# Query pieces two batches ahead, keys one pair earlier, K turned in front of the key additions, in a fused attention and mixture-of-experts kernel

## The chip, the cores and the metric

The kernel runs on one NeuronCore of one Trainium2 chip. The metric is the device time of one execution in microseconds (us): the median of three runs. The profile is of one further execution, taken by the hardware profiler; its span, from the first to the last instruction, is some us shorter than the device time. TensorE is PE in the profile (its weight loads PEld), VectorE is DVE, ScalarE is ACT, GpSimd is POOL, SyncE is SP.

## The reference

Attention with one key and value head for 16 query heads, and then a two-level mixture of experts in which each token takes one expert.

```python
def _attn_ref(q, k, v):                      # q (8,16,384,64), k and v (8,1,384,64), float32
    scores = np.matmul(q, k.transpose(0, 1, 3, 2)) / np.sqrt(64)
    scores = scores - np.max(scores, axis=-1, keepdims=True)
    attn = np.exp(scores)
    attn = attn / (np.sum(attn, axis=-1, keepdims=True) + 1e-09)
    return np.matmul(attn, v)

def _moe_ref(x, w_group, w_expert, w1, w2):  # x (3072,1024); 4 groups of 4 experts; w1, w2 (4,4,1024,1024)
    # g = argmax(x @ w_group), g_w = its softmax weight; e = argmax(x @ w_expert[g]), e_w likewise
    # out[token] = g_w * e_w * relu(x @ w1[g, e]) @ w2[g, e]
```

The rows of x are the tokens: batch times 384 positions, with the 16 heads of 64 laid side by side.

## The kernel before

**Pairs.** Attention is done in 24 pairs `p` of a batch and a block of 128 query positions: `b, st = divmod(p, 3)`, `st` 0, 1 or 2. The loop over `p` (line 501) writes out by hand the order of the instructions of every engine; an engine's instructions run in that order, each when its semaphores allow. I call the work of one turn of the loop the phase of pair p. A phase has three parts.

- *Head*: three key blocks of scores (`scores(p, 0)` to `scores(p, 2)`, line 242: four matmuls of K against Q into a PSUM tile, then one exponential on ACT into a tile `pt`), and `prep_q(p + 1)` (line 238): one DVE transpose that turns the next pair's queries, as they lie in `qraw`, into `qT`.
- *Middle*: for six key blocks `j`, the value matmuls of the pair before (`values(p - 1, j)`, line 280), the scores that remain, the DVE key additions `pre_add` (line 253) that sum the exponentials over key blocks, `join` and `invert` for the reciprocals of the sums, and `stats_q(p)` (line 204) on ACT, which reads `qraw`. After that `weigh(p - 1)` (line 292) multiplies the values by the reciprocals, casts them on POOL to `xbf`, and after a batch's last pair has SP store `xbf` to `x_bf` in DRAM. `fold_keys(p)` (line 260) ends DVE's work on the pair.
- *Fills*: `fill(1)` four times, five times in pairs 8, 12, 16, 20 and 22 (line 554). Each pops one of the 14 expert units of an earlier batch: eight `h_unit`s (line 407: 8 matmuls with `w1`, one ReLU on ACT) and six `y_unit`s (line 415: 8 matmuls with `w2`, one ACT instruction that scales by `gsel` into a tile `y`, one SP store of `y` to the output). `y` has four buffers, so the fifth `y` in a row waits until the first one's store has landed. All these, and the scores, take turns on three PSUM buffers (`ps_s`, `tag="s"`).

**Expert choice.** In the fills of `st == 1` the gate's logits of batch b are made (`gate_a`, `gate_both`), in those of `st == 2` `counts(b, b - 1)` (line 334): two small matmuls, then on DVE `choose_b(b)` (line 349: `top` and its index on line 352, from which POOL requests the batch's expert weights `w1` and `w2`, lines 143 and 357), and `gate_c(b - 1)` (line 389), whose last result `gsel` (line 400) every `y_unit` of batch b - 1 reads. On DVE these stand behind `fold_keys(p)` and `prep_k`, and ahead of the next pair's `prep_q`.

**Transfers of queries and keys.** `load_q(b)` (line 82) takes one of two `qraw` buffers and puts eight pieces of 192 KB on a list `q_todo`; `some_q()` (line 95) requests one. SP requests them on line 89, in runs of 128 bytes. Before the change `load_q(b + 1)` is called at the start of the phase with `st == 0`. Up to p = 3 four pieces go out in the middle of a phase, later one after each fill. So a later batch's first pieces are requested in the fills of `st == 0` and the rest in those of `st == 1`. `prep_q` of that batch's first pair needs all eight, and it stands at the head of the phase with `st == 2`. `load_k(b)` (line 100) requests the keys in four pieces of 48 KB, also in runs of 128 bytes, and `prep_k(b)` (line 228) turns them on DVE into `kT[b]`, which the first scores of the next batch read. Before, keys are requested behind the middle of `st == 1` and turned behind `fold_keys` of `st == 2`. SP has one queue for all of these and for the stores of `y` and `x_bf`; it takes them in the order of the program.

**Tail.** After the last pair, lines 571 to 721 do the remaining expert units and one pair of batch and expert that the choice left out, gathered to at most 128 rows.

Of the kernel before, what the change touches and what calls it, by code (L numbers as in the profile page):

```python
# [21 lines left out]
def kernel(  # L22
# [12 lines left out]
    B, H, S, D = q.shape  # L35
# [6 lines left out]
    ST = S // P  # L42
# [39 lines left out]
    def load_q(b):  # L82
        t = pool.tile([P, HP, NB, 32], FP32, tag="qraw", bufs=2, name="qraw")
        q_raw[b] = t
        n = HP // 2

        def piece(i, a, j):
            hs = slice(i * n, (i + 1) * n)
            nc.sync.dma_start(out=t[64 * a + 32 * j:64 * a + 32 * j + 32, hs].rearrange("p h k d -> p (h k) d"), in_=qv[b, a, j, :, hs].rearrange("i h k d -> i (h k) d"))
        for i in range(2):  # L90
            for a in range(2):
                for j in range(2):
                    q_todo.append(lambda i=i, a=a, j=j: piece(i, a, j))
# [6 lines left out]
    def load_k(b):  # L100
        kt = pool.tile([P, NB, 32], FP32, tag="k", bufs=2, name="k")
        for a in range(2):
            for j in range(2):
                nc.sync.dma_start(out=kt[64 * a + 32 * j:64 * a + 32 * j + 32], in_=kv[b, 0, j])
        k_raw[b] = kt
# [98 lines left out]
    def stats_q(p):  # L204
        junk = pool.tile([P, 2 * CW], BF16, tag="junk", bufs=1, name="junk")
        nc.scalar.activation(out=junk[:].rearrange("p (h n) -> p h n", h=HP), in_=q_of(p), func=ACTF.Square, accum_out=stat_q[:, p:p + 1])  # L206

    def stats_k(b):
        junk = pool.tile([P, 2 * CW], BF16, tag="junk", bufs=1, name="junk")
        nc.scalar.activation(out=junk[:, 0:S], in_=k_raw[b][:].rearrange("p k d -> p (k d)" if b > 0 else "p s a d -> p (s a d)"), func=ACTF.Square, accum_out=stat_k[:, b:b + 1])  # L210
# [8 lines left out]
    def turn_q(p, nat, copies):  # L219
        qT[p] = pool.tile([P, 2 * CW], FP32, tag="qT", bufs=2, name="qT")  # L220
        n = HP // len(copies)
        for i, copy in enumerate(copies):
            ps = side([P, 2 * CW], FP32, "qps")
            for h in range(n):
                nc.tensor.transpose(out=ps[:, h * P:(h + 1) * P], in_=nat(i * n + h).rearrange("p a d -> p (a d)"), identity=ident[:])
            copy(out=qT[p][:, i * n * P:(i + 1) * n * P], in_=ps[:, 0:n * P])

    def prep_k(b):
        kT[b] = pool.tile([P, S], FP32, tag="kT", name="kT")
        nc.vector.transpose(out=kT[b][:], in_=k_raw[b][:].rearrange("p k d -> p (k d)"))  # L230

    def q_of(p):
        b, st = divmod(p, ST)
        if b == 0:
            return q_raw[0][:, st].rearrange("p h a d -> p h (a d)")
        return q_raw[b][:, :, st * (P // 32):(st + 1) * (P // 32)].rearrange("p h k d -> p h (k d)")

    def prep_q(p):
        qT[p] = pool.tile([P, 2 * CW], FP32, tag="qT", bufs=2, name="qT")
        nc.vector.transpose(out=qT[p][:].rearrange("p (h n) -> p h n", h=HP), in_=q_of(p))  # L240

    def scores(p, j):
        b = p // ST
        ps = side([P, 2, CW], FP32, "s")
        for c in range(2):
            for a in range(2):
                r = slice(64 * a, 64 * a + 64)
                nc.tensor.matmul(out=ps[64 * c:64 * c + 64, a, :], lhsT=kT[b][r, j * D:(j + 1) * D], rhs=qT[p][r, c * CW:(c + 1) * CW], start=True, stop=True)  # L248
        t = pool.tile([P, 2, CW], FP32, tag="pt", bufs=9, name="pt")
        nc.scalar.activation(out=t[:], in_=ps[:], func=ACTF.Exp, scale=scale)  # L250
        pt[p, j] = t

    def pre_add(p, j):
        if j == 1:
            presum[p] = pool.tile([P, 2, CW], FP32, tag="presum", bufs=1, name="presum")
            nc.vector.tensor_add(out=presum[p][:], in0=pt[p, 0][:], in1=pt[p, 1][:])  # L256
        else:
            nc.vector.tensor_add(out=presum[p][:], in0=presum[p][:], in1=pt[p, j][:])  # L258

    def fold_keys(p):  # L260
        fold[p] = pool.tile([P, 32], FP32, tag="fold", name="fold")
        nc.vector.tensor_reduce(out=fold[p][:], in_=presum[p][:].rearrange("p a (n i) -> p (a n) i", i=32), axis=AX, op=OP.add, apply_transpose=True)  # L262
    sums = {}

    def join(p):
        sm = side([P, 2, CW], FP32, "sm")
        for c in range(2):
            for a in range(2):
                r = slice(64 * c, 64 * c + 64)
                nc.tensor.matmul(out=sm[64 * a:64 * a + 64, c, 0:16], lhsT=sel2[r].rearrange("p a b -> p (a b)"), rhs=fold[p][r, 16 * a:16 * a + 16], start=True, stop=True)  # L270
        sums[p] = sm
# [8 lines left out]
    def values(p, j):  # L280
        b = p // ST
        if j == 0:
            o_ps[p] = ps_m.tile([P, 2, CW], FP32, tag="o", name="o")
        for c in range(2):
            for a in range(2):
                r = slice(64 * c, 64 * c + 64)
                nc.tensor.matmul(out=o_ps[p][64 * a:64 * a + 64, c, :], lhsT=v_sb[b][r, j, :], rhs=pt[p, j][r, a, :], start=(j == 0), stop=(j == KB - 1))  # L287
# [169 lines left out]
    def fill(n):  # L457
        while n > 0:
            if not units:
                if begun[0] >= B or begun[0] not in wts:  # L460
                    return
                units.extend(first_units(begun[0]))
                begun[0] += 1
            units.pop(0)()
            n -= 1
# [7 lines left out]
    def jobs_gates(b):  # L473
        if b == 0:
            return [lambda: gate_a(0, 0, 1), lambda: choose_a(0, gate_b(0, 0, 1)), lambda: counts(0, None)]
        return [lambda: gate_a(b, 0, ST), lambda: gate_both(b)]
# [24 lines left out]
    for p in range(NP):  # L501
        b, st = divmod(p, ST)
        jobs = jobs_gates(0) if p == 2 else []
        if st == 0 and b + 1 < B:
            load_q(b + 1)
        for j in range(3):
            scores(p, j)
            if p == 0 and j == 0:
                turn_q(1, lambda h: q_raw[0][:, 1, h], [nc.vector.tensor_copy])
        if p == 0:  # L510
            prep_k(1)
        elif 2 < p < NP - 1:
            prep_q(p + 1)
        if jobs:
            jobs.pop(0)()
        if p == ST + 1:
            fill(3)
        for j in (1, 2):
            pre_add(p, j)
        for j in range(KB):  # L520
            if p > 0:
                values(p - 1, j)
            if j == 2 and p > 0:
                join(p - 1)
            if j + 3 < KB:
                scores(p, j + 3)
            if 0 < j < 4:
                pre_add(p, j + 2)
            if j == 2 and p > 0:
                invert(p - 1)  # L530
            if j == 3:
                stats_q(p)
                if p == 1:
                    turn_q(2, lambda h: q_raw[0][:, 2, h], [nc.scalar.copy])
                elif p == 2:
                    turn_q(3, lambda h: q_nat[h // HC][:, h % HC], [nc.scalar.copy])
            if jobs:
                jobs.pop(0)()
            if p <= ST and 0 < j < 5:
                some_q()  # L540
        assert not jobs
        if p > 0:
            weigh(p - 1)
        fold_keys(p)
        if st == 1 and b + 1 < B:
            if b > 0:
                load_k(b + 1)
            load_v(b + 1)
        if st == 2 and b + 1 < B:
            if b > 0:  # L550
                prep_k(b + 1)
            stats_k(b + 1)
        if p > ST:
            n = 5 if p in FIVES else 4
            steps = {}
            if st == 2 and b > 0:
                steps = {0 if b == 1 else 1: lambda: counts(b, b - 1)}
            if st == 1:
                gate_a_, gate_b_ = jobs_gates(b)
                steps = {n - 2: gate_a_, n - 1: gate_b_}  # L560
                if b == B - 1:
                    steps = {1: gate_a_, 2: gate_b_, n - 1: lambda: counts(b, b - 1)}
            if p == NP - 1:
                steps = {1: bound_a, 2: bound_b}
            for i in range(n):
                fill(1)
                some_q()
                if i in steps:
                    steps[i]()
# [256 lines left out]
```

## Time and profile before

| | |
|---|---|
| device time, median of 3 | 499.33 us (499.28 to 500.36) |
| span of the profiled execution | 495.7 us |
| mean granted TensorE clock | 0.985 |
| PE busy | 467.5 us (94%) |
| DVE busy | 304.4 us (61%) |
| ACT busy | 248.0 us (50%) |
| query pieces, 56 of 192 KB | median 5.0 us from request to landing |
| key pieces, 28 of 48 KB | median 3.4 us |
| stores of `y`, 36 of 256 KB | median 5.6 us |
| stores of `x_bf`, 8 of 768 KB | median 7.8 us |
| expert weights | 4 transfers of 512 KB, 10.1 us, and 1 of 2048 KB, 24.2 us, for a batch |

An engine that is busy nearly all the span sets the time, and then its idle stretches are what can be taken away without changing its work. So the table is to be read together with the list of who waited for whom, and with the order in time around each of PE's gaps. Transfers run beside all engines; what counts is what waits for their landing.

### The profile page before, as it was taken

The numbers are of one execution on the slowest core, as the hardware profiler recorded it, in microseconds if no ns is written. First come the engines' busy times: TensorE is split into PE (matmuls) and PEld (weight loads), VectorE is DVE, ScalarE is ACT, GpSimd is POOL, SyncE is SP. The second block draws the span as 40 slices with busy tenths as digits, with TensorE's granted clock in tenths as the row PEclk, the third lists the DMA queues.
The fourth block names the chain that finished last, engine by engine and source line by source line (L and its number), as shares of the span: only waits on it lengthen the run. The fifth ranks groups of instructions, "written<-read, shape, count | busy, mean of one in ns | idle before, by whom it ended". The sixth has DMA issues, their size and how long they took to land. (4 is left out here: it accounts for less than half of the span.)

```text
span 495.7 us, 9385 instructions
## 1 busy us (share of the span) xinstructions
PE 467.5 (94%) x3810; PEld 203.9 (41%) x3828; DVE 304.4 (61%) x479; ACT 248.0 (50%) x355; POOL 60.3 (12%) x82
## 2 busy tenths in 40 slices
PE   8999999999979999697999999899997999999994
PEld 6333343344433343232344434344433434444652
DVE  4999759757397454781678671985449774834210
ACT  3957546554626546253465455455463465423332
POOL 1003000300012000300003000020003101202000
PEclk9999999999999999798999999999999999999998
DMA  9889991699609996299734998089961992994991
GB/s 166 95 108 154 217 184 13 124 243 225 100 2 183 252 188 70 35 199 267 159 33 61 226 240 166 1 137 240 188 128 19 195 212 108 182 223 133 228 242 69
DMA packets 155746, 74.52 MB, mean 150 GB/s; under 512 B 120731, under 2 KB 139163, under 8 KB 155696
## 3 DMA queue, kind: packets, MB, share of 16 engines
q0 software_dynamic: 28512, 37.84, 44.4%
q1 hardware_dynamic: 126384, 35.81, 34.6%
q8 instruction: 32, 0.52, 0.4%
q10 hardware_dynamic: 800, 0.20, 0.2%
q14 instruction: 18, 0.15, 0.1%
HBM read 92.62 MB, written 19.40 MB: 226 GB/s over the span
## 5 line engine op out<-in xcount | busy, mean ns | idle before, releaser
L250 ACT ACTIVATE pt<-s 128x1024 f32<-128x1024 f32 x144 | 141.9, 1026 | 71.3 <-PE s L248 70.1
L248 PE MATMUL s<-qT,kT 64*64 64x512 f32 x1152 | 146.7, 609 | 16.2 <-DVE top L352 12.0
L287 PE MATMUL o<-pt,v 64*64 64x512 f32 x1152 | 142.1, 594 | 0.0
L258 DVE TENSOR_TENSOR presum<-presum,pt 128x1024 f32<-128x1024 f32 x96 | 116.6, 1215 | 16.9 <-ACT pt L250 11.4
L412 PE MATMUL hps<-xbf,w 128*128 128x384 bf16 x512 | 89.0, 326 | 2.2 <-ACT hT L413 1.6
L420 PE MATMUL yps<-w,hT 128*128 128x512 bf16 x367 | 85.6, 379 | 0.9
L287 PEld LDWEIGHTS o<-pt,v 64*64 64x64 f32 x1152 | 44.2, 134 | 77.4 <-issue 77.1
L248 PEld LDWEIGHTS s<-qT,kT 64*64 64x64 f32 x1152 | 40.8, 135 | 79.9 <-issue 52.9
L299 POOL CAST xbf<-xT 128x1024 bf16<-128x1024 f32 x24 | 25.0, 1043 | 355.6 <-DVE xT L298 355.6
L412 PEld LDWEIGHTS <-w 128*128 128x128 bf16 x512 | 48.2, 98 | 47.6 <-issue 18.2
L413 ACT ACTIVATE hT<-hps 128x384 bf16<-128x384 f32 x64 | 31.4, 491 | 70.1 <-PE hps L412 64.7
L256 DVE TENSOR_TENSOR presum<-pt 128x1024 f32<-128x1024 f32 x24 | 29.1, 1211 | 50.8 <-ACT pt L250 50.5
L420 PEld LDWEIGHTS <-hT 128*128 128x128 bf16 x384 | 36.4, 98 | 47.9 <-issue 7.3
L421 ACT ACTIVATE y<-yps,gsel 128x512 f32<-128x512 f32 x36 | 24.4, 687 | 55.5 <-PE yps L420 37.1
L240 DVE STREAM_TRANSPOSE qT<-qraw 128x1024 f32<-128x1024 f32 x20 | 24.5, 1225 | 22.6 <-DMA qraw<-in_q_dram 22.6
L298 DVE TENSOR_TENSOR xT<-o,rinv 128x1024 f32<-128x1024 f32 x24 | 29.2, 1216 | 4.2 <-PE o L287 4.2
L277 DVE STREAM_TRANSPOSE rinv<-rc 128x1024 f32<-128x1024 f32 x24 | 29.9, 1246 | 0.8
L143 POOL DMA_DIRECT2D w<-in_moe_w_dram x36 | 24.8, 707 | 41.9 <-DVE gsel L400 22.0
L262 DVE TRANSPOSE_TENSOR_REDUCE fold<-presum 128x32 f32<-128x1024 f32 x24 | 29.6, 1232 | 0.0
L364 DVE COPY L<-lps 128x20 f32<-128x20 f32 (+1 forms) x16 | 3.0, 186 | 40.6 <-PE lps L318 40.6
L206 ACT ACTIVATE junk<-qraw 128x1024 bf16<-128x1024 f32 x21 | 22.0, 1048 | 0.0
L421 ACT ACTIVATE yt<-yps,gsel 128x512 f32<-128x512 f32 x12 | 8.2, 687 | 15.6 <-PE yps L420 12.0
(147 smaller groups left out, 187.3 us busy)
## 6 DMA issues: line engine op xcount, KB each, us to landing
w<-in_moe_w_dram POOLq DMA_DIRECT2D x36, 512.0 KB, 10.1
w<-in_moe_w_dram POOLq DMA_DIRECT2D x9, 2048.0 KB, 24.2
qraw<-in_q_dram SPq DMA_DIRECT2D x56, 192.0 KB, 5.0
out_dram<-y SPq DMA_DIRECT2D x36, 256.0 KB, 5.6
x_bf<-xbf SPq DMA_DIRECT2D x8, 768.0 KB, 7.8
out_dram<-yt SPq DMA_DIRECT2D x12, 256.0 KB, 6.2
v<-in_v_dram SPq DMA_DIRECT2D x16, 96.0 KB, 2.8
k<-in_k_dram SPq DMA_DIRECT2D x28, 48.0 KB, 3.4
```

The source lines that it names most:

```text
L248: nc.tensor.matmul(out=ps[64 * c:64 * c + 64, a, :], lhsT=kT[b][r, j * D:(j + 1) * D], rhs=qT[p][r, c * CW:(c + 1) * CW], start=True, stop ...
L250: nc.scalar.activation(out=t[:], in_=ps[:], func=ACTF.Exp, scale=scale)
L256: nc.vector.tensor_add(out=presum[p][:], in0=pt[p, 0][:], in1=pt[p, 1][:])
L258: nc.vector.tensor_add(out=presum[p][:], in0=presum[p][:], in1=pt[p, j][:])
L262: nc.vector.tensor_reduce(out=fold[p][:], in_=presum[p][:].rearrange("p a (n i) -> p (a n) i", i=32), axis=AX, op=OP.add, apply_transpose= ...
L277: nc.vector.transpose(out=t[:].rearrange("p (b i) -> p b i", i=32), in_=rc[:].rearrange("p c b -> p (c b)").unsqueeze(2).to_broadcast([P, ...
L287: nc.tensor.matmul(out=o_ps[p][64 * a:64 * a + 64, c, :], lhsT=v_sb[b][r, j, :], rhs=pt[p, j][r, a, :], start=(j == 0), stop=(j == KB - 1))
L298: nc.vector.tensor_mul(out=xT[b][:, :, ts], in0=o_ps[p][:].rearrange("p c (h n) -> p (c h) n", n=P), in1=rinv[p][:].rearrange("p (h n) -> ...
L412: nc.tensor.matmul(out=ps[:, 0:S], lhsT=w1[:, ko, fc * P:(fc + 1) * P], rhs=xb[:, ko, :], start=(ko == 0), stop=(ko == KO - 1))
L413: nc.scalar.activation(out=state["h"][:, fc, :], in_=ps[:, 0:S], func=ACTF.Relu)
L420: nc.tensor.matmul(out=ps[:], lhsT=state["h"][:, fo, st * P:(st + 1) * P], rhs=w2[:, fo, nh * CW:(nh + 1) * CW], start=(fo == 0), stop=(fo ...
L421: nc.scalar.activation(out=y, in_=ps[:], func=ACTF.Copy, scale=gs_of()[:, st:st + 1])
```

## The change

It moves three things and adds no work.

- Queries: batch b + 2 is requested in the phase with `st == 2` of batch b (from the third pair, p = 2, on), in front of that phase's fills, and no longer at the start of batch b + 1's first phase. The buffer it takes is that of batch b, whose last readers are `stats_q` and `prep_q` of that phase and the one before. Only batch 1 is still requested at p = 0. The limit of the middle's requests goes up by one pair, to p = 4.
- Keys: batch b + 1 is requested in front of the fills of `st == 0` (the opening pair), one phase earlier.
- K is turned (`prep_k(b + 1)`) at the head of the phase with `st == 2`, behind `prep_q` and in front of the key additions, and no longer behind `fold_keys`.

It is meant to have queries and keys landed before DVE comes to turn them, and `kT` ready before PE comes to the next batch's first scores.

```diff
-        if st == 0 and b + 1 < B:
-            load_q(b + 1)
+        if p == 0:
+            load_q(1)
         for j in range(3):
             scores(p, j)
...
         elif 2 < p < NP - 1:
             prep_q(p + 1)
+            if st == 2:
+                prep_k(b + 1)
...
-            if p <= ST and 0 < j < 5:
+            if p <= ST + 1 and 0 < j < 5:
                 some_q()
...
         fold_keys(p)
+        if st == 0 and 0 < b < B - 1:
+            load_k(b + 1)
         if st == 1 and b + 1 < B:
-            if b > 0:
-                load_k(b + 1)
             load_v(b + 1)
         if st == 2 and b + 1 < B:
-            if b > 0:
-                prep_k(b + 1)
             stats_k(b + 1)
+            if b + 2 < B:
+                load_q(b + 2)
```

In the built program DVE, ACT, POOL and PE have the same instructions as before, and on DVE only the turning of K stands elsewhere. SP's order changes. In the phases with `st == 0` of batches 1 to 6 it is now the store of `x_bf`, four key pieces, and then stores of `y` and query pieces by turns; before, the keys were behind all of them. In the phases with `st == 2` query pieces stand between the stores of `y`, where there was none.

## The prediction

> **What bounds the kernel.** I read the shares of busy time, then the list of waits, then PE's order in time, and from each PE gap went back to the engine that released it.
>
> ```profile
> PE 467.5 (94%) x3810; PEld 203.9 (41%) x3828; DVE 304.4 (61%) x479; ACT 248.0 (50%) x355; POOL 60.3 (12%) x82
> ...
> q0 software_dynamic: 28512, 37.84, 44.4%
> q1 hardware_dynamic: 126384, 35.81, 34.6%
> ```
>
> PE is the bound, busy nearly always, so its gaps are what can be won. (The queue lines serve below: weights move in packets of 37.84 MB / 28512 = 1327 bytes, what SP requests in 283 on average.) The list of waits says what makes the gaps:
>
> ```profile
> DVE qT L240 <- DMA qraw<-in_q_dram: 22.6, 5, 6.6
> ...
> PE s L248 <- DVE top L352: 12.0, 4, 4.6
> ...
> ACT y L421 <- DVE gsel L400: 9.9, 2, 6.3
> ...
> PE s L248 <- ACT y L421: 3.9, 2, 2.9
> ...
> ACT y L421 <- DMA out_dram<-y: 5.0, 1, 5.0
> ```
>
> PE doesn't wait for queries; DVE does, 22.6 us at L240, and then PE waits for DVE. The wait is put down to `top`, but what scores need is `kT` (L230), just in front of it. Pair 11, DVE and then PE in order of time:
>
> ```profile
> 193.11 1.25 DVE L240 STREAM_TRANSPOSE qT<-qraw 128x1024 f32<-128x1024 f32 x1 [6.57 <-DMA qraw<-in_q_dram]
> ...
> 203.16 1.23 DVE L262 TRANSPOSE_TENSOR_REDUCE fold<-presum 128x32 f32<-128x1024 f32 x1
> 204.32 0.54 DVE L230 STREAM_TRANSPOSE kT<-k 128x384 f32<-128x384 f32 x1
> 204.78 0.14 DVE L352 MAX8 top<-cnt 128x8 f32<-128x16 f32 x1
> ```
>
> ```profile
> 197.53 2.76 PE L412 MATMUL hps<-xbf,w 128*128 128x384 bf16 x16 [0.53 <-ACT hT L413]
> 204.91 5.40 PE L248 MATMUL s<-qT,kT 64*64 64x512 f32 x24 [4.62 <-DVE top L352]
> ```
>
> DVE lost 6.57 us in front of L240, the additions slid behind, and PE stood 4.62 us. Its next 24 matmuls took 5.40 us; the same group takes 2.81 at 250.13. The windows give the reason in the granted clock (the number ahead of the DMA share):
>
> ```profile
> 201.00:205.00 4.00, 0.09 (x4) 0.09 (x8) 3.96 (x7) 0.00 (x0) 1.04 (x1) 0.89 0.00 0
> 205.00:208.00 3.00, 3.00 (x16) 0.95 (x20) 2.25 (x9) 1.02 (x1) 1.72 (x3) 0.50 0.10 8
> ```
>
> From the start of those scores to `join` pair 12 takes 9.91 us (204.91 to 214.82), pair 15 takes 6.92 (250.13 to 257.05): this gap costs another 2.99.
>
> Another kind of gap is at the end of pair 12, where five `y_unit`s come together and the fifth `y` waits for the first one's store. SP in order of time, then the times to landing of three requests of that stretch:
>
> ```profile
> 221.41 0.36 SPq L301 DMA_DIRECT2D x_bf<-xbf  x1
> 221.87 0.38 SPq L442 DMA_DIRECT2D out_dram<-y  x1
> 222.34 0.43 SPq L89 DMA_DIRECT2D qraw<-in_q_dram  x1
> 222.87 7.12 SPq L442 DMA_DIRECT2D out_dram<-y  x1
> ```
>
> ```profile
> x_bf<-xbf SPq DMA_DIRECT2D x1, 768.0 KB, 7.7
> ...
> out_dram<-y SPq DMA_DIRECT2D x1, 256.0 KB, 9.3
> ...
> qraw<-in_q_dram SPq DMA_DIRECT2D x1, 192.0 KB, 11.8
> ```
>
> The store of `x_bf` lands at 229.1, the first `y` at 231.2, the piece at 234.1; ACT evicts the fifth `y` at 231.32 and PE, idle from 229.16, goes on at 232.06. With the low clock behind it pair 13 needs 11.42 us to its `join` (227.21 to 238.63), 4.50 over 6.92.
>
> **What the Trainium skill says.** "TensorE: Matmul & The Clock Gate", Part 1: the array falls to half clock after an idle window of about 3.4 us and needs one as busy to return. The trace agrees: granted 0.50 behind the 4.62 us gap, 1.00 again by 212; but 2.90 us of idleness was enough behind pair 12. "DMA: Bandwidth & Descriptors", Queues, rings and completion order: a DMA engine takes turns between queues packet by packet. This case agrees in kind: beside the weights a query piece of 1536 runs of 128 bytes took 6.8 to 7.2 us behind the `y` ahead of it (pair 6: 113.7 to 120.9; pair 9: 171.8 to 178.6), though it is smaller than `y`. The first page, Architectural detail, has ACT and DVE as strict queues; the slide of DVE at pair 11 shows it.
>
> **The change part by part.**
>
> *Queries early.* Pieces were requested in the fills of `st == 0` and `st == 1`, the last 4 to 8 us before DVE wanted them. Now half go out in the fills of the `st == 2` before, when the DMA share is 0.00 (140 to 146, 194 to 206), the rest in `st == 0`. For pairs 11, 17 and 20 SP's list (store of `x_bf`, keys, at most four `y` or five at pair 12, at most four pieces) then ends around the start of `st == 1` or in its course, and `prep_q` finds its queries. I take DVE's waits of 6.57, 3.50 and 6.24 us to zero. PE gains the gaps: 4.62 + 2.99 at 11, 2.35 at 17, 3.08 at 20: 13.0 us. Behind them PE is fed: `fold_keys` would end at 197.8 at pair 11, PE at 200.3.
>
> Pair 8 is different. DVE's wait of 6.05 costs PE 1.95 (at 144.79) and 1.03 (at 147.83, `y` waiting for `gsel`). Its pieces go out in the fills of pairs 5 and 6, and pair 5's now stand between `y` stores as the weights start (89.8). Three pieces at 7 us hold SP's queue until the weights end, near 121; left then are `x_bf`, keys, three `y`, four pieces: 2.5 MB. Before, 2.2 MB were left there and took 14 us (to 134.95). At 140 to 190 GB/s that is 13 to 17 us, where DVE is ready at 128.9: the wait may stay nearly whole. `gsel` stands behind the same DVE work, `kT` included, wherever K is turned. I take half of 2.98, 1.5; ends 0 and 2.98.
>
> *K turned early.* The same 0.54 us on DVE, moved; what it delays, the first key addition, waits 2 to 6 us for ACT in most phases. It takes the `kT` wait away by itself, but not `gsel`'s. Nothing is added to the sum above.
>
> *Keys early.* They land a phase before they are turned. But four pieces of 48 KB, 1536 runs of 128 bytes like one query piece, now stand between `x_bf` and the first `y` of every `st == 0`, while weights run. I expect this to cost at pair 12. In us from the start of its scores: without the low clock `x_bf` is requested at 16.5 - 3.0 = 13.5 and lands at 13.5 + 7.7 = 21.2. Weights were requested at 1.4 (206.28), the last landing 24.2 after its request at 208.96, at 28.3; DVE being 6.6 earlier and PE 4.6, and K out of the way, it is 2.4 less, 25.9. Keys land at 21.2 + 7 = 28.2, or about 1 after the weights, 26.8: I take 26.8. The first `y` lands 1.5 later, 28.3, the fifth is evicted (0.69) at 29.0. PE runs dry at 229.16 - 204.91 - 2.99 = 21.3. Gap 7.8, low clock 3.0: 10.8 in place of 4.5, a loss of 6.3. Ends: 0 (keys slip through) and 10 (keys in full, `x_bf` later). In other phases no fifth `y` comes so soon behind a first: pairs 15 with 16, and 18 with 19, have a phase between.
>
> *At pair 6* the third `y` needs pair 5's second store, now behind one piece (about 105.5, wanted at 106.8), and the first unit of batch 1 its `w1` at 106.5 (landing then 12.7 us after 90). Both near; I take 0, end 3.
>
> Sum: 13.0 + 1.5 - 6.3 = 8.2 us, 499.33 - 8.2 = 491.1.
>
> **Rivals.**
> - *A, keys and pieces are hidden*: pair 12 stays as it is. 499.33 - 13.0 - 1.5 to 2.98: 483.4 to 484.8. For: `x_bf` in front takes 7.7 us anyway. Against: the 7 us of every piece beside weights.
> - *B, more of the queue's delay comes through*: pair 8 gains nothing, pair 6 loses 2, pair 12 loses 8: 499.33 - 13.0 + 10 = 496.3. For: three pieces ahead of `y` at the weights' start. Against: those stores have a whole phase to land.
> - *C, slower or the same*: `y` stores wait behind keys in pairs 16 and 19 too, 4 us each with the low clock, or pieces still late at pair 20: 499.33 - 13.0 + 10 + 8 = 504; with one of them 500. For: the opening phase's SP list grows by a piece's worth. Against: the margins there, 4 us and more (first `y` of pair 15 lands near 297, its buffer is wanted at 301).
>
> **How the numbers follow.** Main line 0.52, A 0.2, B 0.15, C 0.13. Predicted is the main line, 491.1. The range runs from just above A's dearer end to B with 1 us over it: 485.0 to 497.5. Faster is the main line, A and B, 0.87; C I split into 0.05 same and 0.08 slower.
>
> **What would show it.** Right: L240's waits for `qraw` gone at pairs 11, 17, 20; no PE wait on `top`; one PE gap of some 8 us behind pair 12, released by `y` L421, which waits for its store; granted 0.5 only behind that. A: that gap near 2.9. Wrong: PE gaps released by `y` at pairs 16 or 19, or at L412 of pair 6 by weights, or L240 still waiting at 11, 17 or 20.

## The result, and the profile after

The changed kernel takes 485.02 us (median of 4, 484.5 to 485.75) against 499.3 for the kernel before; the ratio is 0.9714, interval 0.9691 to 0.9737. The forecast was 491.1. The span of the profiled execution went from 495.7 to 482.0 us. The shares of busy time on the page of after:

```profile
span 482.0 us, 9393 instructions
...
PE 463.8 (96%) x3810; PEld 201.5 (42%) x3828; DVE 304.3 (63%) x479; ACT 247.9 (51%) x355; POOL 60.3 (13%) x82
```

The work is the same on every engine. PE is 3.7 us shorter in busy time; some 3.0 of that is low clock, at which PE worked 8.8 us in the middle of the kernel before and 2.7 us now (the last section has the stretches). The list of waits of after (engine, line, what it waited for: us, times, longest):

```profile
ACT y L421 <- DMA out_dram<-y: 12.0, 2, 9.5
...
PE s L248 <- ACT y L421: 7.8, 2, 7.4
...
DVE qT L240 <- DMA v<-in_v_dram: 1.0, 1, 1.0
```

The 22.6 us of DVE at the turning of queries have become 1.0, and PE's wait on `top` is no longer there. What has grown is PE's wait for an eviction of `y`, 3.9 to 7.8 us, with ACT's wait for the store of a `y` behind it, 5.0 to 12.0. (The 1.0 us is put down to `v`, which the instruction doesn't read; the last two query pieces, requested from 123.44 on, just ahead of `v`, and 5.3 us in landing, arrive about then.) PE in order of time has two gaps of over 0.3 us left between the opening pairs and the tail:

```profile
163.66 1.09 PE L248 MATMUL s<-qT,kT 64*64 64x512 f32 x8 [0.44 <-ACT y L421]
...
215.20 1.95 PE L248 MATMUL s<-qT,kT 64*64 64x512 f32 x16
224.53 1.99 PE L248 MATMUL s<-qT,kT 64*64 64x512 f32 x8 [7.38 <-ACT y L421]
```

The large one is behind pair 12. SP in order of time shows the new order there, the store of `x_bf`, then keys, then the first `y`:

```profile
209.39 0.36 SPq L301 DMA_DIRECT2D x_bf<-xbf  x1
209.80 4.85 SPq L104 DMA_DIRECT2D k<-in_k_dram  x4
214.74 0.42 SPq L442 DMA_DIRECT2D out_dram<-y  x1
```

The DMA view of that stretch has 7.6 us to landing for `x_bf`, 11.7 for the keys and, asked by itself, 8.9 for this `y`: 217.0, about 221.5 and 223.6. ACT evicts the fifth `y` at 223.79.

Where the time went is best seen pair by pair. ACT's `stats_q` runs once in the middle of each pair; the table has the time from one to the next, taken from ACT's order of time in each trace, for the pairs in which any two kernels differ by over half a us. The row of pair n holds the fills of pair n - 1 and the first half of pair n. (Experiments, told below: e1 queries early alone, e2 K turned early alone, e3 keys early alone, e4 queries and K, e10 the fifth fill moved from pair 12 to pair 11 in the kernel before, e8 the same in e4.)

| pair | before | after | e1 | e2 | e3 | e4 | e10 | e8 |
|---|---|---|---|---|---|---|---|---|
| 7 | 17.17 | 17.18 | 18.69 | 17.17 | 17.17 | 17.51 | 17.16 | 17.54 |
| 9 | 22.00 | 18.02 | 18.03 | 23.59 | 21.59 | 18.03 | 22.03 | 18.02 |
| 10 | 17.59 | 18.26 | 17.59 | 17.59 | 17.59 | 17.59 | 17.59 | 17.59 |
| 12 | 24.24 | 15.87 | 15.87 | 16.60 | 20.10 | 15.88 | 22.93 | 17.61 |
| 13 | 23.82 | 28.27 | 23.72 | 26.56 | 31.03 | 22.49 | 17.58 | 17.59 |
| 15 | 15.88 | 15.88 | 15.87 | 16.56 | 15.87 | 15.88 | 21.59 | 15.88 |
| 18 | 18.28 | 15.87 | 15.87 | 16.56 | 17.42 | 15.87 | 16.95 | 15.87 |
| 21 | 21.02 | 17.17 | 17.17 | 20.31 | 18.98 | 17.17 | 20.01 | 17.17 |

Before to after: 4.0 us won behind pair 8, 8.4 behind 11, 2.4 behind 17, 3.9 behind 20, 18.6 in all; 4.5 lost behind pair 12 and 0.7 behind pair 9. With 0.2 from the other pairs, the start and the end that is the 13.7 us of the span. The 0.7 is of this profile alone: e9 below is the same program up to pair 10, and its row 10 has 17.59.

### The profile page after: what moved, and what is told of

Same layout as the page of the kernel before. It is cut to its first block, busy times and chain, and to the rows that moved or that the text cites. A ratio compares the mean times of both kernels' runs of the same rounds, so it can differ in the third digit from the quotient of the medians.

```text
span 482.0 us, 9393 instructions
## 1 busy us (share of the span) xinstructions
PE 463.8 (96%) x3810; PEld 201.5 (42%) x3828; DVE 304.3 (63%) x479; ACT 247.9 (51%) x355; POOL 60.3 (13%) x82
## 5 line engine op out<-in xcount | busy, mean ns | idle before, releaser
L248 PE MATMUL s<-qT,kT 64*64 64x512 f32 x1152 | 144.3, 599 | 8.1 <-ACT y L421 7.8
L248 PEld LDWEIGHTS s<-qT,kT 64*64 64x64 f32 x1152 | 39.7, 134 | 70.7 <-issue 46.2
L364 DVE COPY L<-lps 128x20 f32<-128x20 f32 (+1 forms) x16 | 3.0, 185 | 40.5 <-PE lps L318 40.5
```

## The experiments

Each ratio is to the kernel before as it ran beside the experiment. Its median there was 496.4 to 498.2 us and not 499.3, so experiments are compared by their ratios and, pair by pair, by their traces.

**One part at a time.** Each edit is the part of the change's diff that its name says, alone.

*e1, queries early alone:* `load_q` two batches ahead and the limit of the middle's requests, keys and `prep_k` as before.

> Queries early alone; keys requested and turned where they were. Theory (late queries make DVE late, and the early key requests are what lengthens the gap behind pair 12): all PE gaps behind pairs 8, 11, 17 and 20 gone and the gap behind pair 12 no longer than the 2.9 us of before, so 485.0 - 4.5 = 480.5 us. Rival (PE needs kT turned early as well): a wait on the turned keys stays at some pairs, 0.7 to 3 us each, 483 to 488. Rival (the gap behind pair 12 comes from something else than the keys, such as the query pieces or the weights starting sooner): gap 7 us again, 485.

Measured: 479.54 us, ratio 0.9636 (0.9587 to 0.9685). The theory holds. No DVE wait for queries is left, no PE wait on `kT` either though K is still turned behind `fold_keys`, and the gap behind pair 12 is 2.50 us. So neither of the other two parts is needed for the gain.

```profile
109.99 1.95 PE L248 MATMUL s<-qT,kT 64*64 64x512 f32 x16 [1.30 <-ACT y L421]
...
220.52 1.98 PE L248 MATMUL s<-qT,kT 64*64 64x512 f32 x8 [2.50 <-ACT y L421]
```

The first of these, 1.30 us among pair 7's first scores, is new and released by `y`: pair 6's third `y` waits for a store of pair 5 that now has query pieces in front of it. It varies: with queries early row 7 is 17.2 to 18.7 us, and e9, the same program as the whole change up to there, has a gap of 0.63 where the whole change has none.

*e2, K turned early alone:*

```diff
             prep_q(p + 1)
+            if st == 2:
+                prep_k(b + 1)
...
         if st == 2 and b + 1 < B:
-            if b > 0:
-                prep_k(b + 1)
             stats_k(b + 1)
```

> K turned in front of the key additions, alone. Theory A (PE only ever waits for kT at pairs 11, 17 and 20, and gsel is wanted by nobody there): DVE still waits some 22 us for queries, but the gaps of 4.62 (with 2.99 of low clock), 2.35 and 3.08 go, pair 8 stays: 499.3 - 13 = 486 us. Theory B (DVE being late reaches PE by another way, the values' accumulator or the exponentials): the gaps move instead of going, 493 to 499.

Measured: 491.84 us, ratio 0.9883 (0.9839 to 0.9927). Neither expectation: by the ratio it gains 5.8 us (3.6 to 8.0), where theory A had 13. DVE waits 27.5 us for queries in this profile. PE no longer waits for `kT`; PE in order of time shows where the lateness of DVE comes through in its place, here at the end of pair 20:

```profile
368.87 2.76 PE L412 MATMUL hps<-xbf,w 128*128 128x384 bf16 x16 [0.53 <-ACT hT L413]
373.92 1.46 PE L412 MATMUL hps<-xbf,w 128*128 128x384 bf16 x8 [2.29 <-DVE rc L275]
375.31 2.81 PE L248 MATMUL s<-qT,kT 64*64 64x512 f32 x24
```

`rc` is the reciprocal of `invert`. It reads the sums that `join` left in one of the three PSUM buffers, and until DVE comes to it the units have two. DVE's order of time in the same trace has the reason: the turning of queries at 366.80 after 8.91 us of waiting, and `rc` six instructions on, at 373.52. The rest of the missing gain is at pair 9 (23.59 in the table, 1.6 more than before, with gaps as long but a low clock behind them) and behind pair 12, where this profile has a gap of 5.59 us.

*e3, keys early alone:*

```diff
         fold_keys(p)
+        if st == 0 and 0 < b < B - 1:
+            load_k(b + 1)
         if st == 1 and b + 1 < B:
-            if b > 0:
-                load_k(b + 1)
             load_v(b + 1)
```

> Keys requested a phase early, alone. Theory (four key pieces of small runs between the store of x_bf and the first y hold up the fifth y of pair 12): gap behind pair 12 of 7 to 9 us in place of 2.9, the rest as before: 503.5 to 506 us. Rival (keys are hidden): 499.3.

Measured: 497.49 us (20 runs), ratio 1.0004 (0.9979 to 1.0028). The ratio is the rival's, and still the theory's gap is there:

```profile
203.94 2.81 PE L248 MATMUL s<-qT,kT 64*64 64x512 f32 x24 [3.47 <-DVE top L352]
233.96 1.98 PE L248 MATMUL s<-qT,kT 64*64 64x512 f32 x8 [8.75 <-ACT y L421]
...
380.05 2.81 PE L248 MATMUL s<-qT,kT 64*64 64x512 f32 x24 [1.06 <-DVE top L352]
```

Behind pair 12 PE stands 8.75 us in place of 2.90, and the table's row 13 is 7.2 us longer. But DVE's wait at pair 11 is 5.42 us and not 6.57, PE's gap 3.47 and not 4.62 with no low clock behind it (2.81 us for the 24 matmuls, 5.40 before), and rows 9, 12, 18 and 21 are 7.4 us shorter together. That fits the order of SP's list, in which keys are no longer in front of the second half of the query pieces in `st == 1`. Some 3.0 of the 7.4 us and 1.4 of the 7.2 are low clock, which differs from one execution to the next. Keys early are thus not hidden: two effects cancel in the old kernel. With queries early only the loss is left.

*e4, queries and K turned early, keys as before:*

> Queries early and K turned early, keys requested where they were. Theory: as the whole change with pair 12's gap back at 2.9 us or less, 480.5 us. If keys then land too late for the earlier turning: a DVE wait for k at the head of the third pairs, 1 to 4 us each, mostly hidden, 480.5 to 484. Rival (keys don't make pair 12's gap): 485.

Measured: 478.37 us, ratio 0.9623 (0.958 to 0.9666). Pair 12's gap is 2.95 us. Turning K early gains nothing over e1 that the intervals can tell, and early keys are what the change loses: ratio 0.9714 against 0.9623, 485.0 us against 478.4.

**What of the keys costs.** *e5 and e6* take e4 and put four further reads of 48 KB where the early keys stood, into the tile that the keys fill later. e6 reads other, contiguous bytes, which are not used.

```diff
+    def load_more(b):
+        t = pool.tile([P, NB, 32], FP32, tag="k", bufs=2, name="k")
+        for a in range(2):
+            for j in range(2):
+                rows = slice(64 * a + 32 * j, 64 * a + 32 * j + 32)
+                nc.sync.dma_start(out=t[rows], in_=kv[b, 0, j])          # e5: runs of 128 bytes
+                nc.sync.dma_start(out=t[rows].rearrange("p k d -> p (k d)"), in_=kl[b, j])  # e6: 1536
+        k_raw[b] = t
...
         fold_keys(p)
+        if st == 0 and 0 < b < B - 1:
+            load_more(b + 1)
```

> Queries and K turned early, keys requested late, and in the place of the early keys (between x_bf and the first y of the opening pairs) four further reads of 48 KB in runs of 128 bytes into the tile that the keys fill later. Theory (it is these small reads in front of y, beside the weights, that lengthen pair 12's gap): gap 7 to 8 us behind pair 12 again, 483 us. Rival (the whole change's longer gap came from its other order of pieces and stores): 478.4, as without them.

> The same with the four further reads of the same bytes in runs of 1536 bytes (128 in place of 1536 packets; the data read there is not used). Theory (packets count beside the weights, not bytes): the reads take 1 to 2 us there and not 4.5, the gap behind pair 12 is 3 to 5 us, 478.5 to 480.5. Rival (bytes, or the number of requests on SP, count): gap as with the short runs, 483.

*e11* does e6's reads in one request of 128 partitions:

> As with the four further reads in runs of 1536 bytes, but all 192 KB in one request of 128 partitions (the data read there is not used). If bytes beside the weights cost: gap behind pair 12 again near 5.0 us. If SP's requests cost (1.90 us for four): gap 3.3 to 3.7 us. If neither does, and the run before was chance: 2.6 to 3.0 us. The low clock behind it varies from 0.2 to 3 us, so the gap is the measure and not the time: 478 to 484.

The gap behind pair 12, from PE's order of time in the profile of each. e4, without further reads:

```profile
220.67 1.09 PE L248 MATMUL s<-qT,kT 64*64 64x512 f32 x8 [2.95 <-ACT y L421]
```

e5, four reads in runs of 128 bytes:

```profile
224.66 1.98 PE L259 MATMUL s<-qT,kT 64*64 64x512 f32 x8 [7.53 <-ACT y L432]
```

e6, four reads in runs of 1536 bytes:

```profile
222.57 1.99 PE L261 MATMUL s<-qT,kT 64*64 64x512 f32 x8 [4.99 <-ACT y L434]
```

e11, one read in such runs:

```profile
221.60 1.99 PE L258 MATMUL s<-qT,kT 64*64 64x512 f32 x8 [4.84 <-ACT y L431]
```

e5 gives the whole change's gap (7.38), so these reads in this place are its cause. Of the 4.6 us that they add, some 2.0 are there in long runs too, in one request or in four, which leaves the bytes as their cause: bytes that stand in SP's queue beside the weights. This is e11's first expectation; e6 lies between its two, its gap at the top of the theory's 3 to 5 us and its time the rival's. Another 2.5 come with the small runs; the DMA view has 12.0 us to landing for the short reads and 7.7 for the long ones. SP's requests as such don't matter: for four it took 1.90 us and for one 0.43, and the gap is 0.15 us apart. Each gap is of one profile; without reads in that place it was 2.50, 2.64 and 2.95 us (e1, e7, e4), a spread of 0.45. The times are 484.62 us (e5), 483.70 (e6) and 482.66 (e11), their ratios 0.9727 (0.9699 to 0.9755), 0.9715 (0.9683 to 0.9746) and 0.9721 (0.9677 to 0.9764) can't be told apart: they hold the low clock as well, which costs 2.0, 2.4 and 2.7 us in the three profiles, in no order of the gaps' length (the last section has the reason).

*e7, the keys in another place:* the whole change, with the keys behind the fills of the opening pair.

```diff
-        if st == 0 and 0 < b < B - 1:
-            load_k(b + 1)
...
                 if i in steps:
                     steps[i]()
+        if st == 0 and 0 < b < B - 1:
+            load_k(b + 1)
```

> The whole change with the keys requested behind the fills of the opening pair, so still a phase earlier than before, but behind its y stores. Theory (their place in front of y is the cost): gap behind pair 12 at 2.9 us, 478.4 us, no DVE wait for keys. Rival (early keys cost wherever they stand): 482 to 485.

Measured: 478.77 us, ratio 0.9612 (0.9575 to 0.9649), gap 2.64 us:

```profile
220.66 1.09 PE L248 MATMUL s<-qT,kT 64*64 64x512 f32 x8 [2.64 <-ACT y L421]
```

DVE has no wait for keys. They are requested in the same phase, at 228.68 and not at 209.80, and cost nothing: it is the place in front of `y`.

**Doing without the fifth `y`.** *e8, e9, e10* move the fifth fill from pair 12 to pair 11: `FIVES = (8, 11, 16, 20, 22)`. In e8 it is made in e4, in e9 in the whole change, in e10 in the kernel before.

> Queries and K turned early, keys requested late, and the fifth fill moved from pair 12 to pair 11, so that no more than four y come together in pair 12 and the fifth's buffer is one of a phase before. Theory: pair 12's gap of 2.9 us and its low clock (1.6) go, one unit moves to pair 11: 478.4 - 4.5 = 473.9 us. Rival (the store of the y made in pair 11 now stands behind four query pieces, or gsel isn't ready there): a new wait in pair 11 or 12 takes 1 to 4 us back, 475 to 478.

> The whole change (keys early too) with the fifth fill moved from pair 12 to pair 11. Theory (early keys cost only by the y buffer that the fifth y of pair 12 waits for): with no fifth y there, no gap, as fast as the same without early keys, 474.5 us. Rival (early keys cost in other ways too): 476 to 479.

> The kernel before with the fifth fill moved from pair 12 to pair 11, nothing else. Theory (two separate kinds of gap): pair 12's gap and its low clock go, 4.5 us, and pair 11's shrinks by about the 1.7 us that the moved unit keeps PE busy, with less low clock behind it (0 to 3): 490 to 494 us. Rival (the y wait was only hidden behind other waits of pair 12 or 13): 497 to 499.

e8: 474.54 us, ratio 0.9523 (0.9496 to 0.955). From 60 us to the tail, PE's order of time has no gap of over 0.3 us left. e9: 474.50 us, ratio 0.9545 (0.9503 to 0.9588): with no fifth `y` early keys cost nothing that shows. These two are the best of all the kernels here. e10: 495.62 us (20 runs), ratio 0.9984 (0.9962 to 1.0007), outside the expected 490 to 494. The gap behind pair 12 is gone there too (row 13: 17.58), but its trace has a new one behind pair 14. DVE of e10 in order of time:

```profile
251.19 1.25 DVE L240 STREAM_TRANSPOSE qT<-qraw 128x1024 f32<-128x1024 f32 x1 [5.22 <-DMA qraw<-in_q_dram]
...
262.40 0.53 DVE L230 STREAM_TRANSPOSE kT<-k 128x384 f32<-128x384 f32 x1
```

and PE of e10:

```profile
262.99 4.50 PE L248 MATMUL s<-qT,kT 64*64 64x512 f32 x24 [3.27 <-DVE top L352]
```

In the kernel before, pair 14 was the one late pair without a wait for queries. PE's stand behind pair 12 let the pieces catch up: rows 12 and 13 together are 40.5 us in e10, 43.2 in e2, 48.1 before and 51.1 in e3, and DVE's wait at pair 14 is 5.22, 1.44, 0 and 0. (Without the fifth fill pair 12 also requests one piece less and pair 13 one more; but SP had no pause in e10 from 220.53 to the last piece at 245.3, so that order alone doesn't make the last one later.) Take that stand away and pair 14 waits like the others, 5.22 us on DVE, 3.27 on PE, and a low clock (4.50 for 2.81 us): row 15 is 5.7 us longer. What is won at one place is owed at the next, as long as queries are late.

## Why the prediction was right, and where its sizes were off

The forecast was a gain of 8.2 us and the measured one is 14.3. 485.02 lies within the range by 0.02 us: that it does is luck. The mechanism was right, and the sizes were too small for the gain and too large for the loss.

**The bound and the chain** held: PE's gaps at pairs 8, 11, 17 and 20 came from DVE, DVE's lateness from query pieces, and pieces requested a phase sooner take it away. e1 shows that this part is enough. All the signs named as right are there; beside that gap, 0.50 is granted only in the last 2.2 us of the span.

**Pairs 11, 17 and 20** were put at 7.6, 2.35 and 3.08 us, 13.0 together; the table has 8.4, 2.4 and 3.9, 14.6. The surplus is mostly the gaps of 0.53 us on an `h_unit` at pairs 11 and 20, which I had taken to stay. They went in every kernel with queries early. e2's wait on `rc` suggests the late DVE, with its PSUM buffer held, as their cause; I made no test of that.

**Pair 8** is the first mis-sized term: 1.5 us forecast, 4.0 measured. I had let three pieces hold the queue until the weights' end near 121, with 2.5 MB to go. The pieces were as slow as that, or slower (in the trace of after the first two land at 105.4 and 117.2), but the weights' last transfer, requested at 91.89, landed after 25.1 us, at 117.0 and not 121, and the third piece and `x_bf` followed by 118.5 and 120.4. So only 1.7 MB were left (keys, three `y`, four pieces), and they took to 129.6, some 190 GB/s. DVE waited 1.04 us and PE not at all.

**Pair 12** is the second: 6.3 us forecast, 4.5 measured, so the direction and the cause were right. From the start of pair 12's scores (195.88) `x_bf` was requested at 13.5, and `x_bf`, keys and the first `y` landed at 21.1, 25.6 and 27.8, where I had 13.5, 21.2, 26.8 and 28.3. The one step in another order is that the keys landed 0.9 us ahead of the weights' end (222.4) and not behind it. The gap was put at 7.8 and is 7.38; it is the low clock that I over-priced. From the start of the scores to `join` pair 13 takes 15.87 us (215.20 to 231.07), which is 6.92 + 7.38 + 1.57: I had 3.0 for the 1.57, taking it from the one gap over 4 us that the trace of before has. The windows of after show the array at 0.50 while it stands, and 0.96 soon after it goes on, so that most of the low clock lies in the gap, where it costs nothing:

```profile
217.00:221.00 4.00, 0.14 (x4) 0.00 (x0) 0.00 (x0) 0.00 (x0) 0.00 (x0) 0.93 1.23 217
221.00:224.00 3.00, 0.00 (x0) 0.00 (x0) 0.00 (x0) 0.21 (x1) 0.00 (x0) 0.50 1.24 271
224.00:227.00 3.00, 2.47 (x12) 0.80 (x16) 0.66 (x1) 2.73 (x4) 0.00 (x0) 0.50 1.18 263
227.00:230.00 3.00, 3.00 (x32) 1.07 (x28) 1.99 (x3) 1.63 (x2) 0.00 (x0) 0.96 1.11 267
```

**Turning K early** was costed at nothing, and e1 against e4 agrees. **Keys early**: the runs of 128 bytes as the cost is half the story, 2.5 of 4.6 us; the other 2.0 are bytes. **Pair 6** was put at 0 with an end of 3 us: 0 in the whole change's profile, 1.30 us of gap in e1, 0.63 in e9.

**The rivals.** The time, 485.02, is 0.2 us above rival A's dearer end (484.8), but by another way: A wanted the keys hidden, and e4 and e5 show that they are not. Terms of the main line were off on the same side: 2.5 us at pair 8, 1.8 at pair 12, 1.6 at the others; 0.7 lost behind pair 9 in that one profile goes against them.

## What to carry to other kernels

A queue served in order is a schedule: ask of every request moved forward what stands behind it, and who waits for that. In this kernel four small reads ahead of a store cost some 6 us (row 13 of the table, after against e4: 5.8, of which 1.3 are low clock), and nothing when placed behind the stores or when no buffer was short. A part that measures as neutral alone can be a gain and a loss that cancel (e3), and a fix that measures as neutral may only hand its gain to the next wait (e10); compare stage by stage, and try it again once the dominant wait is gone.

## What was not expected of the hardware

The loss behind a PE gap isn't a function of its length. Each trace has the granted clock, and the edges of its low stretches come out of the windows' means: those of after above, 0.93 over the 4 us to 221 and 0.96 over the 3 us from 227, put the fall to 0.50 at 220.44 and the rise at 227.2. In the same way (the loss is what the stretch from the first scores to `join` has over 6.92 us, less the gap where it lies inside):

| gap behind pair | gap, us | clock falls, us from the gap's start | low for, us | of that behind the gap | lost, us |
|---|---|---|---|---|---|
| e1, 12 | 2.50 | 2.48 | 3.41 | 3.39 | 1.9 |
| before, 12 | 2.90 | 2.28 | 3.41 | 2.79 | 1.6 |
| before, 11 | 4.62 | 3.84 | 6.83 | 6.05 | 3.0 |
| e11, 12 | 4.84 | 2.98 | 6.83 | 4.97 | 2.7 |
| e6, 12 | 4.99 | 2.56 | 6.83 | 4.40 | 2.4 |
| after, 12 | 7.38 | 3.29 | 6.83 | 2.74 | 1.6 |
| e5, 12 | 7.53 | 4.36 | 6.83 | 3.66 | 2.0 |
| e3, 12 | 8.75 | 4.04 | 10.24 | 5.53 | 3.0 |
| e7, 12; e4, 12; e3, 11 | 2.64; 2.95; 3.47 | not at all | 0 | 0 | 0.2 at most |

So the loss is half of the low time that lies behind the gap, give or take 0.2 us. The low time is one, two or three times 3.41 us in all of them. Where one trace has two low stretches, their starts lie whole multiples of 3.41 us apart: 27.31 (8 times) before, 78.51 (23) in e2, 58.03 (17) in e10; so does the one in which e1 ends, 256.00 (75) behind its other. In these traces, then, the clock changes on a grid of 3.41 us that stays in place within an execution and lies elsewhere in the next; what a gap of 2.5 us or more costs depends on where it falls on that grid. That is why e1 loses 1.9 us and e4 next to nothing with gaps half a us apart, and the 3.0 us of one gap was no price for another. "TensorE: Matmul & The Clock Gate", Part 1 of the Trainium skill, says that the window by which the clock is set runs freely, without regard to the kernel's start; the grid of these traces agrees. The falls 2.28 to 2.57 us after PE went idle (before, e1, e6) came sooner than after the 3.4 us of idleness that the prediction had.
